# Moving GpSimd's tensor products to VectorE in a fused attention and two feed-forward kernel

## The chip, the cores and the metric

The kernel runs on one core of a Trainium2 chip. The metric is the device time of one execution in microseconds. TensorE does the matrix products, VectorE and GpSimd elementwise work, ScalarE activation functions and copies; SyncE issues most transfers. GpSimd can't read the accumulators (PSUM).

## What is computed

Three stages follow one another. All inputs are float32 (3072 tokens: 4 batches of 768).

```
# 1. a complex-decay recurrence over time, per batch and head (8 heads, D = 48)
scale = min(|a|, 0.999) / (|a| + 1e-6);  a_n = a * scale
S = a_n[t] * S + k[t] (outer) v[t]          # S complex, D x D, k v real
y[t] = q[t] @ real(S)
# 2. a feed-forward: 384 -> 2048 -> 384 with a parametric relu
h = x @ w_in;  x = (max(h, 0) + alpha * min(h, 0)) @ w_out
# 3. top-1 routing to 8 experts, 384 -> 1024 -> 384, relu
logits = x @ w_gate + bias[modality];  e = argmax;  out = p(e) * (relu(x @ w1[e]) @ w2[e])
```

## The kernel before

**Stage 1** is computed in chunks of 128 steps: 6 chunks by 4 batches are 24 steps k. The polar work turns the decay of two steps (a group, 128 partitions by 768 columns) into angles and magnitudes: `polar_group` (line 667). In its words: `ar`, `ai` are the parts of a, `q`, `kk` the queries and keys, and `m2`, `x`, `s`, `e` four work buffers with one slot each, so a new group waits for the slots of the one before. Squares and reciprocal roots (675 to 682), a range test (`ok`, 696 and 697), the arctangent (702), running products and sums over time (`scan`, 723), cosine and sine (748 to 751, tables loaded by ScalarE), then k times the inverse decay (752), q times the decay `pp` (754), and the rows of `z`: for the cosine (r = 0) and the sine (r = 1), k's row on VectorE (763) and q's row (765). `z` is written to DRAM (`zd`) and read back transposed (`qk`). The function `attn` (785) then makes scores (796), masks them (`at`, 798), multiplies with v and with the carried state (814, 816) and writes the transposed result `xt` (821).

Which engine takes an operation is decided by `side(mask)`: a group's `bit` is 1, 2, 4 and 8 for the first four (step 0, step 1, steps 2 and 3, steps 4 and 5) and 16 for all later groups; GpSimd takes the operation where mask and bit have a bit in common, else VectorE. With `GE`, `DQ` and `DZ` at 15, the groups from step 6 on (nine of them) have `ok` (696), q's decay (754) and both of q's rows (765) on GpSimd. For all groups from step 4 on, the cosine's q row is on GpSimd.

**Stage 2** is `moe1` (838): 12 units of 256 tokens, each 8 pairs p of hidden blocks; one pair is a turn g, 96 turns in all. Exactness comes from splitting float32 into an upper part (float32r) and the rest. `l1(g)` multiplies (857 to 860) into `ph`; ScalarE takes a relu (865) into `nf` (in the rows: n), VectorE completes the parametric relu with two instructions (867), ScalarE copies the upper part `gh` (870), and GpSimd makes the lower part `gl` = nf - gh (872). `l2(g - 2)` follows in the same turn: eight matmuls on gh, then four on gl (892), so a gl is read two turns after its first layer. `ph` and `nf` have two buffers, `gh` and `gl` three.

**The order of the work.** At the start a hand-written string orders the first polar groups, the decoding of the weights (`weights_part`, 547) and the first attention steps; in the first 14 turns a second list does so. From then on each unit of stage 2 carries the attention of the unit after it and the polar work of a later one, spread over 5 turns (u below 6) or 7 (later). The polar work of a turn is emitted `behind_turn` (161): `self.paced` holds three instructions of the turn, and with one engine asked for, VectorE's polar instructions are issued after the turn's last 867. What is emitted for the other engines is not held so. The instructions of an engine run in one fixed order that the scheduler of the tile framework chooses from emission order and readiness, not strictly the order of the code. `route` (230) takes the routing along, `ffn_load` (459) the weights of stage 3 (its weight differences are on GpSimd for every third block, `behind_turn` with all three instructions).

**Stage 3** is `moe2` (402), from about 712 us on.

Of the kernel before, what the change touches and what calls it, by code (L numbers as in the profile page):

```python
# [11 lines left out]
F32 = mybir.dt.float32  # L12
F32R = mybir.dt.float32r
BF16 = mybir.dt.bfloat16
I32 = mybir.dt.int32
AF = mybir.ActivationFunctionType
ALU = mybir.AluOpType
# [22 lines left out]
GHB = 3  # L40
# [7 lines left out]
AT = (1, 1, 2, 1, 1, 1, 1)  # L48
RT = ((3, 4), (3, 7))
WORK = "m2", "x", "s", "e"  # L50
XB = 2
PU = 7
KSB = 2
# [18 lines left out]
GB = 0  # L72
GC = 0
GD = 0
DQ = 15
DZ = 15
GE = 15
AS = 5
AE = 7
TM1 = 1  # L80
# [14 lines left out]
class Emit:  # L95
# [25 lines left out]
    def consts(self):  # L121
        nc, cp = self.nc, self.cp
        self.tiny = cp.tile([128, 1], F32, name="tiny")
        nc.vector.memset(self.tiny, 1e-25)
        warm = cp.tile([128, 1], F32, name="warm")
        nc.scalar.activation(warm, self.tiny, AF.Abs_reciprocal_sqrt)
        self.ident = cp.tile([128, 128], F32, name="ident")
        make_identity(nc, self.ident)
        self.mask = cp.tile([128, 128], F32, name="mask")
        nc.gpsimd.memset(self.mask, 1.0)  # L130
        nc.gpsimd.affine_select(
            out=self.mask, in_=self.mask, pattern=[[1, 128]], compare_op=ALU.is_ge,
            fill=0.0, base=0, channel_multiplier=-1,
        )
        self.hpi = cp.tile([128, 1], F32, name="hpi")
        nc.gpsimd.memset(self.hpi, math.pi / 2)
        self.mth = cp.tile([128, 1], F32, name="mth")
        nc.gpsimd.memset(self.mth, -0.56)

        self.first = {}  # L140
        for nm, at0, rest in (("angle", 0.0, 1.0), ("inverse", 1.0, 1e18), ("decay", 1.0, 0.0)):
            t = self.first[nm] = cp.tile([128, 3 * CH], BF16, name=f"first_{nm}")
            nc.gpsimd.memset(t, rest)
            nc.gpsimd.memset(t[:, ::CH], at0)
        self.carry = cp.tile([128, B, 3], F32, name="carry")
        self.magic = cp.tile([128, 1], F32, name="magic")
        nc.gpsimd.memset(self.magic, MAGIC)

        self.oks = cp.tile([128, NSTEP], F32, name="oks")
        nc.gpsimd.memset(self.oks, 2.0 * 3 * CH)  # L150
        self.pend = cp.tile([128, NSTEP, 3], F32, name="pend")
        self.state = cp.tile([96, B * H * D + 16], F32, name="state")
        nc.gpsimd.memset(self.state[:, B * H * D:], 0.0)
        self.al1 = cp.tile([128, NFC], F32, name="al1")
        one = self.one = cp.tile([128, 1], F32, name="one")
        nc.gpsimd.memset(one, 1.0)
        self.mhalf = cp.tile([128, 1], F32, name="mhalf")
        nc.gpsimd.memset(self.mhalf, -0.5)
        self.ones = one.to_broadcast([128, CH])
# [507 lines left out]
    def polar_group(self, ks, wa, wq, work, inline):  # L667
        nc, ap_ = self.nc, self.ap_
        c = ks[0] // B
        ar, ai, q, kk = wa[:, :, 0], wa[:, :, 1], wq[:, :, 0], wq[:, :, 1]  # L670
        m2, x, s, e = work
        V, G, A = nc.vector, nc.gpsimd, nc.scalar
        bit = {0: 1, 1: 2, 2: 4, 4: 8}.get(ks[0], 16)
        side = lambda mask: G if mask & bit else V
# [24 lines left out]
        yield 1  # L699
        V.scalar_tensor_tensor(s, e, 3.0, s, ALU.subtract, ALU.mult)  # L700
        yield 1
        A.activation(ai, ai, AF.Arctan)
        early = ks[0] < 4
        def scaled(bit, out, x, scale, bias):
# [133 lines left out]
    def moe1(self, units, emit_out, before=lambda g: None, after=lambda g: None, order=None, bank=None):  # L838


        nc, ap_, ps = self.nc, self.mp, self.ps
        gs, accs, xts = {}, {}, {}
        w1 = lambda fc, h, c: self.w[fc][:, h, 128 * c:128 * c + 128]
        order = order or [(j, p) for j in range(len(units)) for p in range(NP)]
        bank = bank or (lambda j, t: (ps, "acc", 2))

        def l1(g):
            j, p = order[g]
            u = units[j][0]
# [14 lines left out]
            nf = ap_.tile([128, 2, 256], F32, name=f"n{u}_{p}", tag="n", bufs=2)  # L864
# [3 lines left out]
                    nf[:, i, :], nf[:, i, :], self.al1[:, 2 * p + i:2 * p + i + 1], ph[:, i, :], ALU.mult, ALU.add).ins  # L868
            gh = ap_.tile([128, 2, 256], F32R, name=f"gh{u}_{p}", tag="gh", bufs=GHB)
            copy = nc.scalar.copy(gh, nf).ins  # L870
            gl = ap_.tile([128, 2, 256], F32R, name=f"gl{u}_{p}", tag="gl", bufs=GHB)
            rest = nc.gpsimd.tensor_tensor(gl, nf, gh.bitcast(F32), ALU.subtract).ins  # L872
            if self.pacing:
                self.paced = paced, copy, rest
            gs[g] = (gh, gl)

        def l2(g):
            j, p = order[g]
            u = units[j][0]
            if p == 0:  # L880
                accs[j] = []
                for t in range(2):
                    pool, tag, bufs = bank(j, t)
                    accs[j].append(pool.tile([128, 512], F32, name=f"acc{u}_{t}", tag=tag, bufs=bufs))
            acc = accs[j]
            gh, gl = gs.pop(g)
            pieces = [(t, i, gh, h) for i in range(2) for t in range(2) for h in range(2)]
            pieces += [(t, i, gl, 0) for i in range(2) for t in range(2)]
            if p == NP - 1 and TM1:
                pieces.sort(key=lambda x: x[0])  # L890
            for t, i, x, h in pieces:
                nc.tensor.matmul(acc[t][:, :XW], x[:, i, 128 * t:128 * t + 128], self.w[2 * p + i][:, h, DM:],  # L892
                                 start=(p == i == h == 0 and x is gh), stop=(p == NP - 1 and i == 1 and x is gl))

        n = len(order)
        for g in range(n + LAG):
# [3 lines left out]
            if g >= LAG:  # L900
                l2(g - LAG)
                j, p = order[g - LAG]
# [492 lines left out]
```

## Time and profile before

| | us |
|---|---|
| three runs | 945.52, 948.34, 954.92 |
| median | 948.34 |
| the profiled execution | 951.42 |
| its span, first to last instruction | 949.6 |

The profile is of one execution on this core. Busy time of an engine is the time covered by its instructions; PE is TensorE (PEld its weight loads), DVE VectorE, ACT ScalarE, POOL GpSimd, SP SyncE. Matmuls overlap in their pipeline, so a duration of one is longer than the distance to the next. "Idle before <-X" is how long the engine had nothing to do before an instruction, and which instruction released it. The granted clock (PEclk) is 1.00 at 2.4 GHz and 0.50 at 1.2 GHz.

### The profile page before, as it was taken

The numbers are of one execution on the slowest core, as the hardware profiler recorded it, in microseconds if no ns is written. First come the engines' busy times: TensorE is split into PE (matmuls) and PEld (weight loads), VectorE is DVE, ScalarE is ACT, GpSimd is POOL, SyncE is SP. The second block draws the span as 40 slices with busy tenths as digits, with TensorE's granted clock in tenths as the row PEclk, the third lists the DMA queues.
The fourth block names the chain that finished last, engine by engine and source line by source line (L and its number), as shares of the span: only waits on it lengthen the run. The fifth ranks groups of instructions, "written<-read, shape, count | busy, mean of one in ns | idle before, by whom it ended". The sixth has DMA issues, their size and how long they took to land.

```text
span 949.6 us, 16186 instructions
## 1 busy us (share of the span) xinstructions
PE 838.5 (88%) x5948; PEld 798.2 (84%) x5948; DVE 649.6 (68%) x1268; ACT 479.2 (50%) x870; POOL 397.9 (42%) x335
## 2 busy tenths in 40 slices
PE   0767969889889899998989998989999999999994
PEld 0656958878889899998989998989998879899993
DVE  7878886896779595969687877924555644435551
ACT  7744556664655464655554656422334433434550
POOL 2003543436355346454635464532443335334550
PEclk9856988889899999999999999999999999999997
DMA  8728400444562722425252526150214455435560
GB/s 316 251 83 278 149 10 1 146 118 105 139 180 65 180 65 78 149 71 171 61 142 94 149 70 174 65 105 26 79 41 135 117 169 167 132 109 180 178 195 19
DMA packets 61289, 117.81 MB, mean 124 GB/s; under 512 B 10200, under 2 KB 39400, under 8 KB 61200
## 3 DMA queue, kind: packets, MB, share of 16 engines
q1 hardware_dynamic: 57232, 106.91, 38.2%
q0 software_dynamic: 3968, 9.77, 3.3%
q8 instruction: 49, 0.80, 0.4%
q14 instruction: 40, 0.33, 0.1%
HBM read 85.58 MB, written 28.91 MB: 121 GB/s over the span
## 4 chain that ended last, share of the span: by engine, by line
PE 38%; DVE 20%; DMA 12%; issue 11%; POOL 5%; ACT 4%; SPq 0%; POOLq 0%; DVEq 0%; ACTq 0%
PE acc L892 7%; DMA qk<-zd 7%; PE a2s L498 6%; DMA zd<-z 4%; PE ph L857 3%; PE pa L796 3%; PE ph L858 3%; DVE n L867 3%; PE ph L860 3%; DVE z L763 2%; PE p2s L483 2%; PE p2s L479 2%; PE p2s L480 2%; POOL gl L872 1%; POOL wq L754 1%
## 5 line engine op out<-in xcount | busy, mean ns | idle before, releaser
L872 POOL TENSOR_TENSOR gl<-n,gh 128x512 fp32r<-128x512 f32 x96 | 150.9, 1573 | 208.1 <-ACT gh L870 100.3
L857 PE MATMUL ph<-xt,w 128*128 128x256 f32 x576 | 159.9, 304 | 14.2 <-DVE n L867 12.4
L892 PE MATMUL acc<-w,gh 128*128 128x392 f32 x768 | 160.5, 347 | 0.0
L858 PE MATMUL ph<-xt,w 128*128 128x256 f32 x576 | 153.3, 293 | 0.0
L867 DVE SCALAR_TENSOR_TENSOR n<-n,al,ph 128x256 f32<-128x256 f32 x192 | 84.3, 474 | 97.2 <-ACT n L865 96.9
L892 PEld LDWEIGHTS acc<-w,gh 128*128 128x128 f32 x768 | 134.8, 191 | 0.8 <-issue 0.7
L857 PEld LDWEIGHTS ph<-xt,w 128*128 128x128 f32 x576 | 115.6, 201 | 16.6 <-DVE n L867 7.0
L858 PEld LDWEIGHTS ph<-xt,w 128*128 128x128 f32 x576 | 115.7, 201 | 0.2 <-issue 0.2
L860 PE MATMUL ph<-xt,w 128*128 128x256 f32 x576 | 105.3, 293 | 4.1 <-DVE w L560 4.1
L870 ACT CAST gh<-n 128x512 fp32r<-128x512 f32 x96 | 59.4, 618 | 86.1 <-DVE n L867 71.1
L860 PEld LDWEIGHTS ph<-xt,w 128*128 128x128 f32 x576 | 87.2, 200 | 4.5 <-DVE w L560 4.3
L892 PE MATMUL acc<-w,gl 128*128 128x392 f32 x384 | 87.7, 344 | 3.1 <-POOL gl L872 3.0
L865 ACT ACTIVATE n<-ph 128x512 f32<-128x512 f32 x96 | 56.8, 592 | 61.3 <-PE ph L860 54.1
L796 PE MATMUL pa<-qk 96*128 96x128 f32 x384 | 58.7, 301 | 23.2 <-DMA qk<-zd 20.8
L796 PEld LDWEIGHTS pa<-qk 96*128 96x128 f32 x384 | 54.3, 212 | 27.1 <-issue 21.8
L892 PEld LDWEIGHTS acc<-w,gl 128*128 128x128 f32 x384 | 70.1, 190 | 3.7 <-POOL gl L872 3.7
L798 DVE TENSOR_TENSOR at<-pa,mask 128x512 f32<-128x512 f32 x48 | 32.6, 680 | 25.9 <-PE pa L796 19.8
L584 POOL TENSOR_TENSOR w<-of,w 128x8 fp32r<-128x8 f32 x16 | 10.1, 652 | 92.6 <-ACT w L583 92.6
L487 DVE SCALAR_TENSOR_TENSOR hls<-p2s,hhs 128x512 fp32r<-128x512 f32 x32 | 22.0, 688 | 38.5 <-ACT hhs L486 38.5
L814 PE MATMUL py<-at,v 128*64 128x128 f32 x384 | 43.6, 300 | 3.3 <-DVE at L798 3.3
L468 DVE TENSOR_TENSOR wls<-wrs,whs 128x768 fp32r<-128x768 f32 x20 | 28.6, 1432 | 25.6 <-ACT whs L467 25.6
L261 POOL DMA_INDIRECT tbl<-tok,ix x24 | 24.9, 1037 | 49.7 <-DVE ix L259 43.3
(333 smaller groups left out, 2023.4 us busy)
## 6 DMA issues: line engine op xcount, KB each, us to landing
zd<-z SPq DMA_DIRECT2D x24, 771.0 KB, 3.7
qk<-zd SPq DMA_DIRECT2D x24, 771.0 KB, 7.0
wraw<-in_w_io_dram SPq DMA_DIRECT2D x16, 768.0 KB, 11.9
wrs<-in_wcat_dram SPq DMA_DIRECT2D x32, 384.0 KB, 3.2
wrf<-in_wcat_dram SPq DMA_DIRECT2D x24, 384.0 KB, 3.8
wa<-in_pa__dram SPq DMA_DIRECT2D x10, 768.0 KB, 4.5
wq<-in_pq__dram SPq DMA_DIRECT2D x10, 768.0 KB, 9.6
v<-in_vv_dram SPq DMA_DIRECT2D x24, 200.0 KB, 4.9
```

The lines of the kernel that those rows point to most:

```text
L498: nc.tensor.matmul(acc[t], x[:, 128 * t:128 * t + 128], w[:, DM:], start=(f == 0 and x is hh and w is wh), stop=(last and x is hl))
L796: nc.tensor.matmul(pa[:, i, :], kt[:, h, :], qt[:, h, :CH], start=True, stop=True)
L798: self.last = nc.vector.tensor_tensor(at, pa, self.mask.unsqueeze(1).to_broadcast([128, 4, CH]), ALU.mult).ins
L814: nc.tensor.matmul(o, v[:, h * D:h * D + 64], ats[g][:, i, :], start=True, stop=(c == 0))
L857: nc.tensor.matmul(ph[:, i, :], w1(fc, 0, c), xt[:, c, 0, :], start=(c == 0), stop=False)
L858: nc.tensor.matmul(ph[:, i, :], w1(fc, 0, c), xt[:, c, 1, :], start=False, stop=False)
L860: last = nc.tensor.matmul(ph[:, i, :], w1(fc, 1, c), xt[:, c, 0, :], start=False, stop=(c == 2)).ins
L865: nc.scalar.activation(nf, ph, AF.Relu, scale=-1.0)
L867: paced = nc.vector.scalar_tensor_tensor(nf[:, i, :], nf[:, i, :], self.al1[:, 2 * p + i:2 * p + i + 1], ph[:, i, :], ALU.mult, ALU.add).ins
L870: copy = nc.scalar.copy(gh, nf).ins
L872: rest = nc.gpsimd.tensor_tensor(gl, nf, gh.bitcast(F32), ALU.subtract).ins
L892: nc.tensor.matmul(acc[t][:, :XW], x[:, i, 128 * t:128 * t + 128], self.w[2 * p + i][:, h, DM:], start=(p == i == h == 0 and x is gh), sto ...
```

## The change

It has four parts. `gl` of a turn is made on VectorE instead of GpSimd, and one turn later, behind the two 867 of the next turn; the last one is made in `l2`. `self.paced` then holds this late `gl`, so VectorE's polar work stands behind it. `GE`, `DQ` and `DZ` are 31, which takes `ok`, q's decay and the sine's q row to VectorE in the nine later groups; the cosine's q row stays on GpSimd. Every second group, from step 6 on, uses the slots of `s` and `e` the other way round. And ScalarE evaluates a sine of one column into a scratch tile just ahead of the arctangent.

```
+TURNED = "m2", "x", "e", "s"
...
-DQ = 15
-DZ = 15
-GE = 15
+DQ = 31
+DZ = 31
+GE = 31
...
+        self.trig = cp.tile([128, 1], F32, name="trig")
...
-        m2, x, s, e = work
+        m2, x, s, e = (work[WORK.index(t)] for t in (TURNED if ks[0] // 2 % 2 and ks[0] > 3 else WORK))
...
+        A.activation(self.trig[:, :1], ai[:, 0, :1], AF.Sin)
         A.activation(ai, ai, AF.Arctan)
...
+        late = []
+        def lower(engine, g, nf, gh, u, p):
+            gl = ap_.tile([128, 2, 256], F32R, name=f"gl{u}_{p}", tag="gl", bufs=GHB)
+            gs[g] = (gh, gl)
+            return engine.tensor_tensor(gl, nf, gh.bitcast(F32), ALU.subtract).ins
...
             copy = nc.scalar.copy(gh, nf).ins
-            gl = ap_.tile([128, 2, 256], F32R, name=f"gl{u}_{p}", tag="gl", bufs=GHB)
-            rest = nc.gpsimd.tensor_tensor(gl, nf, gh.bitcast(F32), ALU.subtract).ins
+            rest = None
+            if True:
+                parts = late.pop() if late else None
+                late.append((g, nf, gh, u, p))
+                if parts:
+                    paced = lower(nc.vector, *parts)
+                rest = paced
+            else:
+                rest = lower(nc.gpsimd, g, nf, gh, u, p)
             if self.pacing:
                 self.paced = paced, copy, rest
-            gs[g] = (gh, gl)

         def l2(g):
+            if g not in gs:
+                lower(nc.vector, *late.pop())
```

## Rows read from the trace of the kernel before

**Rows 1.** The page's busy times: engine, busy us, share of the span, instructions.

```profile
PE 838.5 (88%) x5948; PEld 798.2 (84%) x5948; DVE 649.6 (68%) x1268; ACT 479.2 (50%) x870; POOL 397.9 (42%) x335
```

**Rows 2.** TensorE's waits, 250 to 712 us: total us, times, longest.

```profile
PE pa L796 <- DMA qk<-zd: 19.6, 7, 3.7
PE py L814 <- DVE at L798: 3.3, 1, 3.3
```

**Rows 3.** Stretches of 50 us: PE, PEld, DVE, ACT, POOL busy, PEclk, DMA.

```profile
150.00:200.00 50.00, 42.04 (x264) 40.48 (x264) 44.33 (x57) 33.76 (x57) 17.66 (x15) 0.86 0.33 95
250.00:300.00 50.00, 46.27 (x391) 44.88 (x390) 41.22 (x69) 29.94 (x53) 24.82 (x18) 0.97 0.45 123
600.00:650.00 50.00, 46.61 (x364) 45.44 (x363) 27.04 (x63) 16.64 (x32) 22.05 (x16) 0.97 0.32 77
```

**Rows 4.** The same view over one unit of eight turns.

```profile
413.80:463.50 49.70, 47.12 (x373) 46.10 (x375) 38.41 (x77) 28.59 (x49) 24.49 (x20) 0.97 0.42 117
```

**Rows 5.** The chain that ended last, 417 to 431 us: start, us, what.

```profile
417.43 1.64 DVE z L763
...
419.22 3.51 DMA zd<-z
...
422.75 7.79 DMA qk<-zd
```

**Rows 6.** Timeline of TensorE, 409 to 431 us: start, us, instruction, idle before.

```profile
409.02 0.52 PE L860 MATMUL ph<-xt,w 128*128 128x256 f32 x3
...
417.29 0.88 PE L892 MATMUL acc<-w,gl 128*128 128x392 f32 x4
...
430.68 1.51 PE L796 MATMUL pa<-qk 96*128 96x128 f32 x8 [2.58 <-DMA qk<-zd]
```

**Rows 7.** Timeline of GpSimd, 408 to 431 us.

```profile
408.62 1.96 POOL L872 TENSOR_TENSOR gl<-n,gh 128x512 fp32r<-128x512 f32 x1 [4.69 <-issue]
410.55 1.82 POOL L754 TENSOR_TENSOR wq<-wq,m 128x768 f32<-128x768 f32 x1
...
429.42 1.27 POOL L872 TENSOR_TENSOR gl<-n,gh 128x512 fp32r<-128x512 f32 x1 [0.89 <-DVE n L867]
```

**Rows 8.** Line 872, 80 to 230 us: ns min/median/max, first and last start.

```profile
L872 POOL TENSOR_TENSOR gl<-n,gh x17: 1279/1869/5390, 84.7 to 229.3; 128x512 fp32r<-128x512 f32 x17
```

**Rows 9.** ScalarE's waits, 250 to 620 us: total us, times, longest.

```profile
ACT m L676 <- POOL wq L754: 14.1, 7, 2.2
```

**Rows 10.** Timeline of ScalarE, 413 us.

```profile
413.16 0.58 ACT L865 ACTIVATE n<-ph 128x512 f32<-128x512 f32 x1
```

**Rows 11.** Timeline of VectorE, 413 to 432 us.

```profile
413.84 0.87 DVE L867 SCALAR_TENSOR_TENSOR n<-n,al,ph 128x256 f32<-128x256 f32 x2 [3.76 <-ACT n L865]
414.63 1.59 DVE L752 TENSOR_TENSOR wq<-wq,s 128x768 f32<-128x768 f32 x1
...
428.50 0.95 DVE L678 TENSOR_TENSOR m<-m,e 128x768 f32<-128x768 f32 x1
429.48 2.02 DVE L684 TENSOR_TENSOR e<-wa,x 128x768 f32<-128x768 f32 x1
```

**Rows 12.** VectorE by line, 413.8 to 463.5 us: busy us, mean ns, idle before.

```profile
L763 DVE TENSOR_TENSOR z<-wq,x 128x384 f32<-128x384 f32 x2 | 2.2, 1092 | 0.0
...
L711 DVE SCALAR_TENSOR_TENSOR m<-m,s 128x768 f32<-128x768 f32 x1 | 1.9, 1917 | 0.0
```

**Rows 13.** VectorE by line, 0 to 84 us.

```profile
L763 DVE TENSOR_TENSOR z<-p,p 128x384 f32<-128x384 f32 x4 | 2.2, 546 | 0.0
```

**Rows 14.** TensorE's waits, 100 to 250 us.

```profile
PE ph L857 <- DVE n L867: 12.4, 4, 3.8
PE acc L892 <- POOL gl L872: 3.0, 1, 3.0
```

**Rows 15.** Timeline of ScalarE, 23 us.

```profile
23.00 1.28 ACT L750 ACT_TABLE_LOAD   x1
```

**Rows 16.** Timeline of VectorE, 25 us.

```profile
24.95 0.56 DVE L763 TENSOR_TENSOR z<-wq,e 128x384 f32<-128x384 f32 x1 [1.26 <-ACT e L750]
```

## The prediction

> **What bounds the kernel now.** I read the page's busy shares first: TensorE's matmuls are busy 838.5 us of the 949.6 us span [rows 1], more than any other engine. TensorE leads, so a change on VectorE and GpSimd can only pay where TensorE stands still or runs at its lower clock. The second view is TensorE's waits by releaser. From 250 to 712 us, where the first feed-forward and the attention run interleaved, nearly all of its idle time has one name: the score matmuls waiting for the transfer qk, 19.6 us in seven waits, the longest 3.7; one more wait of 3.3 us is for the masked scores on VectorE [rows 2]. The third view, stretches of 50 us, shows a granted clock of 0.97 in six of the nine between 250 and 700 us, the first and the last of the six in [rows 3]: after such a stop the engine runs some microseconds at 1.2 GHz, then at 2.4 again. 0.03 of 50 us is 1.5 us of lost work, six times: 9 us.
>
> The fourth view, one period of eight turns (a unit: two steps of attention), gives the load: in 49.7 us TensorE is busy 47.1, VectorE 38.4, GpSimd 24.5 [rows 4].
>
> **Why qk is late.** The chain of waits ends with the last z row on VectorE (417.43 to 419.07), the write of z to DRAM (3.51) and the read back (7.79), and then the scores [rows 5]. TensorE started them at 430.68 after 2.58 idle, so it stood still from 428.10 [rows 6]. Why does that z row end at 419? GpSimd computes q's decay (L754) from 410.55 to 412.37, and only after the gl (L872) that was in front of it, 1.96 long where the shortest takes 1.28 [rows 7, 8]. ScalarE's first square of the next group (L676) writes into the buffer that L754 reads, so it waits for it, and behind it in ScalarE's queue stands the relu of the next turn, which starts at 413.16 although its ph was complete at 409.54 (409.02 plus 0.52) [rows 6, 10]. The two n instructions of that turn follow at 413.84, and behind them, by the pacing edge, k's product at 414.63 and the z rows [rows 11]. That wait of ScalarE on L754 comes seven times between 250 and 620 us, 14.1 us in all and 2.2 at most [rows 9].
>
> **The change, part by part.** All sums are against the profiled execution, 951.4 us with 949.6 in the span; the median of the three runs is 948.3, so 3.1 comes off at the end.
>
> *q's decay on VectorE.* L754 now stands behind the n pair and k's product on VectorE, so the next group's square can no longer be queued in front of a relu that L754 itself waits behind. The relu starts at about 409.6, the n pair ends 1.5 later (as 413.16 to 414.63 did) at 411.1, the late gl at 411.7. Then k's product and q's decay, 0.87 apart each (a product of 768 columns left alone takes 0.95, and neighbours overlap by 0.08, as the n pair from 413.84 for 0.87 and its follower at 414.63 do [rows 11]), three rows of z at 0.47, and a microsecond because GpSimd keeps q's first row: z is complete at about 415.8 instead of 419.07, 3.3 us earlier. Of seven waits of at most 3.7 that removes nearly all; but the margin over the 2.58 is only 0.7, so I leave 2.6 standing: minus 17. With the stops go their half-clock stretches: minus 7 of the 9. What is late next is VectorE itself, so of the 3.3 on the masked scores I take 1.
>
> *What VectorE pays.* A 128x512 product of two SBUF operands is not in its trace. It lies between 0.55 (384 columns) and 0.95 (768) [rows 11, 13], by interpolation 0.68, 0.60 apart in a queue. A unit gets eight of them (4.8), the range test's product and q's decay (0.87 each), two q rows (0.47 each): plus 7.5 us. Against it, GpSimd's operations stretch VectorE's today: L684 takes 2.02, L711 1.92, L763 with the sine 1.09 twice [rows 11, 12], while a product of the same size left alone takes 0.95 and 0.55: 1.07 + 0.97 + 1.09 = 3.1 us a unit. Rows of the same kind that I don't count stand against the GpSimd work that stays (q's first rows, the state product, one scaling). So 38.4 + 7.5 - 3.1 = 42.8 us, while the unit would shrink to some 45.7 (49.7 less 2.6 and 1.5): 94% busy, now 77%. It fits, but an instruction that TensorE needs is behind more of a queue. The late gl, done at about 411.7 in the turn above, is read by matmuls that start at 417.29 today [rows 6]: 5.6 us of cover, some two less in a turn without attention work. A polar turn in which VectorE falls further behind than that stops TensorE. The late gl also frees n's buffer: the relu two turns on waits for it on ScalarE, with the copy gh and the polar activations queued behind, and the polar work of a turn is held behind the gl as well. I charge half a microsecond for each of eight to nine units: plus 4 (bounds 0, and the whole of rival C).
>
> *The start, before 230 us.* There VectorE decodes the weights and is the engine that others wait for: 44.3 of 50 us at 150 to 200 [rows 3]; TensorE waits 12.4 us for n in four places and 3.0 for a gl on GpSimd [rows 14]. The 3.0 goes. The 17 gl that start before 230 [rows 8] put 17 x 0.60 = 10.2 us more on VectorE; it counts fully only where TensorE waits for n, with one or two gl in front of each of the four waits, so I take 4 between minus 10 (if each of the 17 now delays VectorE by as much as it would cost it) and plus 10.2.
>
> *After 712 us* the second feed-forward has no gl; only its first weight differences on GpSimd lose their place behind gl: 0.
>
> *The tiny sine ahead of the arctangent.* Today each group loads a table before the arctangent and another before the sine, 1.28 us each. At the start one such load stands on the path: ScalarE loads at 23.00, and VectorE's first z row waits 1.26 for the cosine [rows 15, 16]. If one table holds both, that is minus 1.3; if the arctangent evicts the sine's, one more load comes in each group, and ScalarE, busy 28.6 of 49.7 [rows 4], hides it except at the start, plus 1.3. No row tells which, so I take 0. *The swapped buffers* of every other group let the next group's first square start before the last z row; only ScalarE gains, which is not the limit: 0.
>
> Sum: -17 - 7 - 1 + 4 - 3 + 4 = -20, so 931.4 for an execution like the profiled one and about 928 for the median.
>
> **Two rules of the notes.** VectorE's L684 took 2.02 us from 429.48, where the product of the same size just before it took 0.95 [rows 11], and GpSimd ran a gl from 429.42 for 1.27 [rows 7]. The Trainium skill, "SBUF — State Buffer", section "Who interferes with whom", says that a VectorE instruction with two SBUF inputs and a GpSimd instruction that reads SBUF exclude each other for the whole instruction. The trace agrees. By that rule alone every removed gl would free VectorE, and the 7.5 would be met by more than the 3.1 that I count.
> Against the change speaks the Trainium skill, "Perfetto Trace Analysis", section "Optimizing Scalar/DVE Operations": where VectorE is saturated, work may go from it to other engines. At 42.8 of 45.7 us it is nearly so here; what this would do in this kernel is rival C.
>
> **The rivals.**
> *A, everything goes.* All 19.6 of the qk waits, all 9.0 of the clock, 3.3 for the masked scores, 3.0 for the gl, and no new wait: 34.9, so 916.5, or 913 on the median's scale. For it: the waits are all of one kind, and none is longer than 3.7. Against: a margin of 0.7 us.
> *B, the transfer comes no earlier.* The late gl, the extra product and the extra row in front of z eat the 3.3 us, or another ScalarE instruction takes the square's place ahead of the relu. Then only the start counts: -3 + 4, so 952, or 949. For it: the order on an engine is the scheduler's, and no row shows the new one.
> *C, VectorE becomes the bound, slower.* If its instructions stay as long as they are, a unit holds 38.4 + 7.5 = 45.9 us of VectorE. It stands idle 11.3 of 49.7 today, waiting on relus and scores; if half of that stays, the unit takes 51.5, 1.8 more, nine times 16; the start pays 10.2 and gains 3.0. Plus 23: 974, or 971. It decides from about 44 us of VectorE per unit. For it: 44.3 of 50 us in the start already. Against: 3.1 us of stretched instructions in three rows.
>
> **How the numbers follow.** The forecast has 0.47 (own range 918 to 937), A 0.20, B 0.21, C 0.12. One per cent of 948 is 9.5 us, about what a measurement of this kernel can tell from no change. Forecast and A are faster by more: 0.67; B is the same: 0.21; C slower: 0.12. The range goes from A less its unknowns (half of the 10 at the start, 1.3 of the table) at 906 up to B plus its table load and the 3.0 if that wait stays too, 953; C is left out.
>
> **What would show it.** Right: no wait of TensorE on qk above 1 us between 250 and 640, a clock of 1.00 in most stretches of 50 us, the relu at the end of a polar group starting within 0.3 us of its ph, L684 and L711 near 1 us, VectorE at 41 to 44 us per unit, GpSimd under 8. Wrong: waits of TensorE on n or gl that total more than 10 us after 250; the waits on qk still there; L684 still at 2 us without a gl beside it.

## The result and the profile after

The changed kernel takes 910.25 us (median of four runs, 907.61 to 912.2) where the kernel before, in the same comparison, takes 946.93: a ratio of 0.960 [0.953, 0.966] (in brackets, here and below, the 95% interval). The forecast was 928, or 0.979. The profiled execution after is 910.59 us with a span of 908.8, against 951.42 and 949.6. The line numbers move: in after the relu is L878, the pair on n L880, gl L858, k's product L757, q's decay L759, the rows of z L768 and L770, the scores L801.

Busy times of after, which answer to [rows 1]:

```profile
PE 819.3 (90%) x5948; PEld 780.0 (86%) x5948; DVE 662.5 (73%) x1400; ACT 467.4 (51%) x871; POOL 205.7 (23%) x203
```

GpSimd's work is halved, VectorE's grows by only 13 us although 132 instructions came to it, and TensorE does the same work in 19 us less: it runs less at its lower clock. 7.7 of these lie ahead of its first turn (28.43 and 20.75 in the first lines of the windows below).

TensorE's waits of after from 250 to 712 us, as in [rows 2]; it is the only row that the view has:

```profile
PE pa L801 <- DMA qk<-zd: 11.4, 4, 5.6
```

The waits on qk fall from 19.6 to 11.4 us, the 3.3 us for the masked scores are gone, and no wait on n or gl came in their place.

To see where the rest comes from, the two spans are cut at the same events: the first product of ph in turns 0, 16, 28 and 80 of the first feed-forward, and its end. Columns as in [rows 3]. First the kernel before:

```profile
0.00:63.60 63.60, 28.43 (x174) 26.32 (x175) 48.63 (x80) 40.32 (x74) 4.93 (x31) 0.83 0.69 241
63.60:223.00 159.40, 128.73 (x878) 120.83 (x878) 131.77 (x205) 90.54 (x171) 66.13 (x56) 0.84 0.35 107
223.00:304.90 81.90, 73.57 (x580) 70.96 (x580) 69.03 (x123) 48.55 (x84) 40.16 (x28) 0.94 0.51 136
304.90:629.00 324.10, 304.08 (x2463) 295.91 (x2461) 246.96 (x495) 174.90 (x299) 160.65 (x124) 0.98 0.41 113
629.00:711.10 82.10, 81.79 (x606) 79.55 (x604) 38.13 (x137) 26.16 (x47) 29.54 (x25) 0.98 0.19 52
```

The same stretches of after:

```profile
0.00:56.20 56.20, 20.75 (x175) 19.24 (x175) 50.00 (x82) 41.12 (x79) 4.90 (x31) 0.98 0.78 273
56.20:206.40 150.20, 125.85 (x876) 117.80 (x877) 131.02 (x213) 85.62 (x167) 26.40 (x36) 0.86 0.37 114
206.40:286.60 80.20, 73.39 (x581) 70.04 (x582) 71.43 (x150) 48.82 (x86) 16.28 (x14) 0.94 0.55 136
286.60:589.30 302.70, 296.90 (x2465) 290.29 (x2462) 253.34 (x574) 166.93 (x295) 52.54 (x42) 1.00 0.47 124
589.30:669.30 80.00, 80.00 (x605) 78.10 (x604) 41.62 (x153) 26.38 (x47) 10.42 (x10) 1.00 0.15 44
```

Turns 28 to 80 give 21.4 us: TensorE's idle time there goes from 20.0 (324.10 less 304.08) to 5.8, and its clock from 0.98 to 1.00, by which its busy time falls by 7.2. Turns 0 to 16 give 9.2. The 7.4 us ahead of turn 0 are not put down to the change: the clock of that stretch (0.83 and 0.98) follows none of its parts. Of the kernels below two, only_masks and only_pair, take about as long as the kernel before (63.2 and 64.3 us to turn 0), while the other sixteen take 55.9 to 58.8, among them only_decay and load_more, which have little or nothing of the change. The second feed-forward is unchanged (238.4 and 239.4 us). Turns 28 to 80 are therefore the stretch by which the experiments are read: nothing of the start is in it. Each such window is of one execution, and executions of one kernel differ (the kernel before took 937.5 to 952.9 us in thirteen of them), so a few us in one window show a cause only together with the ratio.

### The profile page after: what moved, and what is told of

The parts are those of the page before. It is cut to its first block, busy times and chain, and to the rows that moved or that the text cites. A ratio compares the mean times of both kernels' runs of the same rounds, so it can differ in the third digit from the quotient of the medians.

```text
span 908.8 us, 16009 instructions
## 1 busy us (share of the span) xinstructions
PE 819.3 (90%) x5948; PEld 780.0 (86%) x5948; DVE 662.5 (73%) x1400; ACT 467.4 (51%) x871; POOL 205.7 (23%) x203
## 4 chain that ended last, share of the span: by engine, by line
PE 51%; DVE 14%; DMA 10%; issue 4%; ACT 1%; POOL 1%; SPq 0%; POOLq 0%; DVEq 0%; ACTq 0%
PE acc L913 12%; PE a2s L500 6%; DMA qk<-zd 5%; PE ph L870 4%; PE ph L871 4%; PE ph L873 4%; DMA zd<-z 3%; PE pa L801 3%; PE p2s L485 2%; PE p2s L481 2%; DVE n L880 2%; PE p2s L482 2%; PE pu L833 2%; PE py L819 1%; PE a2t L500 1%
## 5 line engine op out<-in xcount | busy, mean ns | idle before, releaser
L870 PE MATMUL ph<-xt,w 128*128 128x256 f32 x576 | 155.3, 298 | 9.7 <-DVE n L880 5.0
L871 PE MATMUL ph<-xt,w 128*128 128x256 f32 x576 | 149.6, 288 | 0.0
L870 PEld LDWEIGHTS ph<-xt,w 128*128 128x128 f32 x576 | 112.0, 194 | 11.6 <-DVE n L880 5.5
L880 DVE SCALAR_TENSOR_TENSOR n<-n,al,ph 128x256 f32<-128x256 f32 x192 | 84.0, 473 | 43.9 <-ACT n L878 43.8
L871 PEld LDWEIGHTS ph<-xt,w 128*128 128x128 f32 x576 | 112.2, 195 | 0.2 <-issue 0.2
L873 PE MATMUL ph<-xt,w 128*128 128x256 f32 x576 | 103.2, 288 | 3.5 <-DVE w L562 3.5
L878 ACT ACTIVATE n<-ph 128x512 f32<-128x512 f32 x96 | 56.9, 593 | 72.0 <-PE ph L873 69.9
L858 DVE TENSOR_TENSOR gl<-n,gh 128x512 fp32r<-128x512 f32 x96 | 66.4, 691 | 30.2 <-ACT gh L883 29.4
L873 PEld LDWEIGHTS ph<-xt,w 128*128 128x128 f32 x576 | 84.7, 195 | 3.7 <-DVE w L562 3.7
L263 POOL DMA_INDIRECT tbl<-tok,ix x24 | 27.4, 1141 | 200.7 <-DVE ix L261 191.0
L801 PE MATMUL pa<-qk 96*128 96x128 f32 x384 | 55.2, 288 | 15.0 <-DMA qk<-zd 13.1
L801 PEld LDWEIGHTS pa<-qk 96*128 96x128 f32 x384 | 51.5, 201 | 18.3 <-DMA qk<-zd 8.6
L500 PE MATMUL a2s<-whs,hhs 128*128 128x384 f32 x128 | 43.7, 341 | 0.0
L500 PE MATMUL a2s<-wls,hhs 128*128 128x384 f32 x128 | 43.5, 340 | 0.0
L469 ACT CAST whs<-wrs 128x768 fp32r<-128x768 f32 x32 | 26.3, 833 | 32.3 <-PE a2s L500 15.8
```

Source lines behind the costliest of these rows:

```text
L263: nc.gpsimd.indirect_dma_start(out=self.tbl, out_offset=bass.IndirectOffsetOnAxis(ap=ix, axis=0), in_=self.tok[:, c, b, :], in_offset=None ...
L500: nc.tensor.matmul(acc[t], x[:, 128 * t:128 * t + 128], w[:, DM:], start=(f == 0 and x is hh and w is wh), stop=(last and x is hl))
L801: nc.tensor.matmul(pa[:, i, :], kt[:, h, :], qt[:, h, :CH], start=True, stop=True)
L858: return engine.tensor_tensor(gl, nf, gh.bitcast(F32), ALU.subtract).ins
L870: nc.tensor.matmul(ph[:, i, :], w1(fc, 0, c), xt[:, c, 0, :], start=(c == 0), stop=False)
L871: nc.tensor.matmul(ph[:, i, :], w1(fc, 0, c), xt[:, c, 1, :], start=False, stop=False)
```

## The experiments

Each kernel below is the kernel before with one part added, or the changed kernel with one part undone. "28 to 80" is the time from TensorE's first product of ph in turn 28 to that in turn 80 (before 324.1, after 302.7); "qk" is TensorE's wait on qk from 250 to 712 us (before 19.6, after 11.4). The two don't always go together: only_gl has short waits on qk and a long stretch, load_more waits as little as only_sine and takes 5.8 us more.

| kernel | ratio to before | qk | 28 to 80 |
|---|---|---|---|
| only_sine | 0.987 [0.981, 0.993] | 13.9 | 311.4 |
| load_early | 0.992 [0.988, 0.995] | 13.2 | 311.7 |
| load_more | 1.000 [0.995, 1.004] | 13.5 | 317.2 |
| only_gl | 0.990 [0.986, 0.995] | 6.5 | 320.4 |
| only_masks | 1.004 [1.000, 1.007] | 20.6 | 322.8 |
| only_decay | 1.008 [1.003, 1.014] | 20.3 | 320.5 |
| decay_held | 0.995 [0.991, 1.000] | 15.1 | 311.5 |
| only_pair | 0.980 [0.975, 0.985] | 13.5 | 311.2 |
| less_sine | 0.974 [0.968, 0.980] | 13.6 | 308.7 |
| less_gl | 0.990 [0.983, 0.998] | 17.3 | 316.5 |
| less_masks | 0.981 [0.975, 0.987] | 9.4 | 311.9 |
| less_turned | 0.967 [0.961, 0.973] | 7.3 | 302.8 |
| same_turn | 1.006 [1.002, 1.010] | 26.8 | 328.1 |
| same_free | 0.977 [0.972, 0.983] | 11.9 | 304.4 |
| all_rows | 0.952 [0.946, 0.958] | 3.4 | 300.2 |
| rows_scale | 0.952 [0.946, 0.958] | 3.9 | 300.7 |
| after_held | 0.965 [0.957, 0.972] | 6.9 | 299.4 |
| rows_held | 0.953 [0.946, 0.961] | 3.5 | 299.4 |

### The sine ahead of the arctangent

```
+        A.activation(self.trig[:, :1], ai[:, 0, :1], AF.Sin)
         A.activation(ai, ai, AF.Arctan)
```

Added alone to the kernel before:

> The kernel before with the tiny sine ahead of the arctangent and nothing else of the change. Theory S (the sine decides the start): each group has two table loads in place of three, the first scores start 1.2 us earlier, and because TensorE is then busy a little sooner its clock stays at 2.4 GHz past 42 us, where it fell to 1.2 before; the relu of turn 0 starts at about 68 us in place of 76.1, and the time falls by 8 us (ratio 0.991). Rival T (a load is worth itself): two loads in place of three, 1.3 us, the clock of the start as before, turn 0 at about 75, ratio 0.998 to 1.000.

Undone in the changed kernel:

> The changed kernel without the tiny sine. Theory S: the start is as in the kernel before, turn 0 at about 76 us, clock down from 42 us on; 8 us slower than the changed kernel, ratio to the kernel before 0.969. Rival T: 1 to 2 us slower than the changed kernel, ratio 0.962.

Alone it gives 1.3 per cent, and its loss takes 1.4 points from the change (0.974 against 0.960). The table loads of the kernel before ahead of the arctangent (L702) and the cosine (L750), over the whole run:

```profile
L702 ACT ACT_TABLE_LOAD x12 | 15.4, 1283 | 0.2
L750 ACT ACT_TABLE_LOAD x12 | 15.4, 1283 | 0.2
```

With the sine (L706 in only_sine) one row stands for both:

```profile
L706 ACT ACT_TABLE_LOAD x12 | 15.4, 1283 | 0.2
```

Alone, the gain is not at the start. Turn 0 does begin 6.8 us earlier, as the first theory had it, but so it does in kernels without the sine (55.9 in only_decay, 56.4 in less_sine); turns 0 to 16 take 160.5 us with it and 159.4 without, while turns 28 to 80 lose 12.7. In the changed kernel turns 28 to 80 take 6.0 us less by it and turns 0 to 16 4.2 (308.7 and 154.4 in less_sine, 302.7 and 150.2 after). The place is the end of a polar group. ScalarE of the kernel before (timeline):

```profile
402.22 0.83 ACT L748 ACTIVATE e<-x 128x768 f32<-128x768 f32 x1
...
403.43 1.28 ACT L750 ACT_TABLE_LOAD   x1
404.73 0.94 ACT L750 ACTIVATE e<-e,hpi 128x768 f32<-128x768 f32 x1
405.57 0.83 ACT L751 ACTIVATE x<-x 128x768 f32<-128x768 f32 x1
406.31 0.57 ACT L865 ACTIVATE n<-ph 128x512 f32<-128x512 f32 x1
```

The same group with the sine alone added:

```profile
393.66 0.83 ACT L753 ACTIVATE e<-x 128x768 f32<-128x768 f32 x1
...
394.76 0.94 ACT L755 ACTIVATE e<-e,hpi 128x768 f32<-128x768 f32 x1
395.60 0.83 ACT L756 ACTIVATE x<-x 128x768 f32<-128x768 f32 x1
396.33 0.58 ACT L878 ACTIVATE n<-ph 128x512 f32<-128x512 f32 x1
```

From the Abs to the relu of the turn it was 4.09 us and is 2.67: the load stood in ScalarE's queue ahead of a relu. The load itself costs the 1.30 from its start to the cosine's. The Trainium skill, "ScalarE: Activation LUTs", section "What ACT_TABLE_LOAD costs", puts a drain of about 1.38 us on top of it, which this trace doesn't show. Behind that relu stand the pair on n (406.91), ScalarE's copy gh (done at 408.49) and the gl at 408.62 [rows 7], which stood in front of the decay; from there the chain is that of the prediction's account. The five waits on qk between 350 and 600 us fall from 12.4 to 6.4 us in all.

Is it that a load is gone, or where it stood? Two kernels ask. load_early has the sine behind the arctangent, with three loads as before, and load_more another activation ahead of the cosine, with a fourth:

```
         A.activation(ai, ai, AF.Arctan)
+        A.activation(self.trig[:, :1], ai[:, 0, :1], AF.Sin)
```

```
+        A.activation(self.trig[:, :1], e[:, 0, :1], AF.Abs_reciprocal_sqrt)
         A.activation(cs, e, AF.Sin, bias=self.hpi, scale=-2.0 * PI_LO)
```

> The kernel before with the sine of one column just behind the arctangent in place of ahead of it: three table loads a group as before, but the last of them is moved from ahead of the cosine to behind the arctangent, some turns earlier. If the place of the load ahead of a turn's relu is what costs, this gains as much as the sine ahead of the arctangent did (0.987): a ratio of 0.982 to 0.994, with turns at the end of a polar group 1.3 to 1.4 us shorter. If the number of loads counts, nothing: 0.996 to 1.004.

> The kernel before with a reciprocal root of one column just ahead of the cosine: ScalarE loads a table more in each group (the one of the root between the arctangent's and the sine's), 1.28 us each, four loads a group in place of three. If what the sine ahead of the arctangent brought (0.987) is the place of one load in ScalarE's queue, this costs as much the other way: a ratio of 1.008 to 1.02, and the waits of TensorE on qk after 250 us grow above 20 us. If the load was covered and the sine's gain was the start alone, 0.998 to 1.005.

load_early keeps three loads, moves one some turns ahead, and gains the same 12 us in turns 28 to 80: there the place counts, not the number. As a ratio it gives 0.8 per cent where the sine gives 1.3; the intervals overlap, so that the missing load is worth something too is not excluded. load_more was to cost as much and cost nothing. Its ScalarE:

```profile
399.81 1.28 ACT L751 ACT_TABLE_LOAD   x1
401.10 0.20 ACT L751 ACTIVATE trig<-e 128x1 f32<-128x1 f32 x1
401.32 1.28 ACT L753 ACT_TABLE_LOAD   x1
402.62 0.84 ACT L753 ACTIVATE x<-x 128x768 f32<-128x768 f32 x1
403.37 0.58 ACT L867 ACTIVATE n<-ph 128x512 f32<-128x512 f32 x1
403.84 0.93 ACT L752 ACTIVATE e<-e,hpi 128x768 f32<-128x768 f32 x1
```

The scheduler put the cosine behind the relu: the relu comes 4.77 us after the Abs (398.60), 0.68 more than before, and not 1.5 more. So the cost could only be half of what was expected; but a relu that is later still should have cost something, and turns 28 to 80 take 6.9 us less than before. This run doesn't confirm the account by the load's place, and why it is not dearer is open. The account rests on only_sine, less_sine and load_early.

### The decay, the masks and the order on SP's queue

The decay alone, and (only_masks) DZ and GE at 31 with it:

```
-DQ = 15
+DQ = 31
```

> The kernel before with q's decay alone on VectorE for the nine later groups. Theory M: this one product holds the square, the relu and so the z rows, so it gives most of what the three products give: 12 us less (ratio 0.987), no wait of ScalarE's first square on it. Rival P: 2 us or less (ratio 0.998 to 1.002).

> The kernel before with the range test's product, q's decay and the sine's q row on VectorE for the nine later groups, gl left on GpSimd. Theory M: the wait of ScalarE on the decay is gone, most of the waits of TensorE on qk (19.6 us from 250 to 712 us) with it; 16 us less (ratio 0.983). Rival P: gl still excludes VectorE, which has more to do now; between no change and 6 us less (ratio 0.994 to 1.000).

ScalarE's wait on GpSimd's decay [rows 9] is gone in both, as the forecast had it, and the waits on qk stay at 20 us. In only_decay the first step's z does come earlier. SyncE's issues in the kernel before, around the chain of [rows 5]:

```profile
419.22 0.32 SPq L662 DMA_DIRECT2D zd<-z  x1
420.46 1.53 SPq L823 DMA_DIRECT2D xt<-t  x2
422.75 0.33 SPq L662 DMA_DIRECT2D qk<-zd  x1
423.20 0.46 SPq L662 DMA_DIRECT2D zd<-z  x1
```

and in only_decay, where the scores begin at 429.75 in place of 430.68:

```profile
416.10 0.32 SPq L664 DMA_DIRECT2D zd<-z  x1
417.56 1.54 SPq L827 DMA_DIRECT2D xt<-t  x2
419.32 0.59 SPq L664 DMA_DIRECT2D zd<-z  x1
420.01 6.83 SPq L664 DMA_DIRECT2D qk<-zd  x2
```

The first write starts 13.65 us ahead of the scores, before 11.46. The second step's z is ready early too, and its write goes ahead of the first step's read back, where before it was issued 0.45 us behind it. Of the chain's last pieces in only_decay

```profile
420.01 9.61 DMA qk<-zd
```

is 1.8 us longer than the 7.79 of [rows 5]. In the mean of the last six groups of turns 28 to 80 it is less: from the first write's start to the read back's end 12.0 us before, 13.0 in only_decay. A kernel with the old order forced onto that queue tests this: the read back of the first step is emitted first, and the second write and the load of wq are issued after it.

```
-BB = 1
+BB = 0
...
-        self.dma(zd.rearrange("h (p c) t -> (h p) (c t)", c=6), z.rearrange("p c j t -> p (c j t)"))
+        with self.tc.issue_after(self.back) if self.back and k % 2 else nullcontext():
+            self.dma(zd.rearrange("h (p c) t -> (h p) (c t)", c=6), z.rearrange("p c j t -> p (c j t)"))
...
```

> The kernel before with q's decay alone on VectorE (1.008, 20.3 us of waits on qk), and on SP's queue the order that the kernel before shows: write of the first step's z, its read back qk, then the second step's write and the load of wq. In the run without this order the first z was complete 2.5 us earlier against the turns, but the second step's write went ahead of the read back, and the way from z to the scores took 13.68 us in place of 11.62. If this sharing is what ate the gain, the waits on qk fall below 12 us and the ratio is 0.980 to 0.995; if not, the waits stay near 20 us and the ratio between 1.00 and 1.015.

The waits fall to 15.1 us only, but the mean way from write to read back is 12.3 us, the ratio goes from 1.008 to 0.995, and turns 28 to 80 from 320.5 to 311.5. Windows of only_decay, then of decay_held:

```profile
304.90:625.40 320.50, 303.61 (x2464) 295.30 (x2462) 253.01 (x496) 175.97 (x298) 153.71 (x117) 0.98 0.45 117
```

```profile
300.50:612.00 311.50, 299.26 (x2464) 290.83 (x2461) 252.42 (x488) 174.37 (x298) 154.85 (x117) 1.00 0.42 117
```

So by these windows the decay on VectorE is worth 12.6 us of that stretch, and the order on SP took back 9.0 of it. Clear of noise is the order (1.008 [1.003, 1.014] against 0.995 [0.991, 1.000]); whether the second write or the load of wq does it is not told apart, as the edit moves both. Against the kernel before the ratio shows little of the 12.6, because turns 16 to 28 take 88.1 us here (87.5 in only_decay) and 81.9 before. Part of the way can stay long even so: in one group, with no second write ahead of it, the read back is issued 5.98 us after the first write (406.41 and 412.39), in the kernel before 3.53. These runs leave that open. In the changed kernel the second write is again issued ahead of the read back:

```profile
391.19 0.51 SPq L664 DMA_DIRECT2D zd<-z  x1
```

Its chain of waits there:

```profile
387.30 0.56 DVE z L770
...
388.01 8.46 DMA zd<-z
...
396.54 6.96 DMA qk<-zd
...
403.63 0.46 PE pa L801 x2
```

From the last row of z (387.86) to the scores it is 15.8 us; before it was 11.6. Here it is the first write that is longer, 8.46 us against 3.51, not the read back, and the order is not enough to explain it: of the 16 parts in which that write lands, the trace has 14 by 391.44, when the second write had only just been issued, and the last two at 393.38 and 396.48. The old order was tried here as well:

> The changed kernel with that same order on SP's queue. Its first z is complete 9.08 us ahead of the scores' turn, where it was 4.61, but the way to the scores took 15.77 us. With the order held it should take about 11.6 again, so that the waits on qk after 250 us (11.4 us in four) go but for the one near 259: a ratio of 0.950 to 0.960, 0 to 1 per cent under the changed kernel. If the waits are not from the order, 0.957 to 0.966.

The waits fall from 11.4 to 6.9 us, the mean way from 13.3 to 12.1, and the time doesn't (0.965 [0.957, 0.972] against 0.960). With no second write ahead of the read back the first write still takes 6.8 to 7.3 us in three of the last six groups. Why the last parts of a write land late in some groups is open.

### gl and the masks together

only_gl adds the late gl alone, only_pair the late gl and the masks. The other two undo a part of the changed kernel, less_gl by the first edit and less_masks by the second:

```
-            if True:
+            if False:
```

```
-DQ = 31
-DZ = 31
-GE = 31
+DQ = 15
+DZ = 15
+GE = 15
```

> The kernel before with the lower parts of the first layer on VectorE one turn later and nothing else of the change. Theory M (q's decay on GpSimd makes qk late): the decay stays on GpSimd, but no gl is in front of it any more, so about a third to a half of the 19.6 us of waits on qk goes; in the decoding stretch from turn 9 to 23 the waits for GpSimd and the stretched instructions go, 8 us; total 14 us less (ratio 0.985). Rival P (GpSimd and VectorE exclude each other, and that is all there is): nearly the whole gain, 25 us or more (ratio under 0.974).

> The changed kernel with gl on GpSimd in its own turn as before; the masks, the swapped buffers and the sine stay. Theory M: 8 from the start (sine) and 16 from the masks remain, ratio to the kernel before 0.975; the stretch from turn 9 to 23 takes as long as before. Rival P: 8 from the start and at most 6 more, ratio 0.986 or above.

> The changed kernel with the range test's product, q's decay and the sine's q row back on GpSimd. Theory M: the waits on qk are back in part (8 to 12 us from 250 us on), ratio to the kernel before 0.976. Rival P: gl is gone from GpSimd, so next to nothing is lost, ratio 0.964.

> The kernel before with two parts of the change together: the lower part gl on VectorE one turn later, and the three masks at 31. No sine, buffers not swapped. Alone the first gave a ratio of 0.990 and the second 1.0035, which multiply to 0.994. If the parts act by themselves, the ratio is 0.99 to 1.00 and TensorE's waits on qk after 250 us stay above 6 us. If GpSimd must be left by both at once, the ratio is 0.965 to 0.98, that of the whole change without the sine (0.974), and the waits on qk after 250 us are below 6 us in all.

Alone they give 0.990 and 1.004, together 0.980: the parts don't add. Undone in the changed kernel they cost 3.0 points (gl) and 2.1 (the masks). With gl still on GpSimd (only_masks), VectorE's rows of z are stretched by gl and by the q row behind it. The sine's q row, which is new on VectorE, as min/median/max ns of 14, in only_masks and then in only_pair:

```profile
L769 DVE TENSOR_TENSOR z<-wq,x x14: 546/961/1657, 304.1 to 616.4; 128x384 f32<-128x384 f32 x14
```

```profile
L769 DVE TENSOR_TENSOR z<-wq,x x14: 547/552/1377, 301.5 to 597.0; 128x384 f32<-128x384 f32 x14
```

The first write of z is longer in only_masks too, 5.3 to 6.6 us in its last six groups (3.51 in [rows 5]); its cause is not shown. With the masks at 15 and gl gone (only_gl), ScalarE waits 17.2 us for GpSimd's range test product (8.0 before) and 10.1 for its decay (14.1 before) from 250 to 620 us, and TensorE gets waits for the masked scores, 13.8 us in 16 (4.2 in two before). Only when both leave is VectorE mostly left alone. Mean durations of three of its instructions in turns 28 to 80 of the kernel before:

```profile
L726 DVE TENSOR_TENSOR_SCAN s<-first_inverse,s 128x384 f32<-128x384 bf16 x12 | 17.1, 1466 | 0.0
L684 DVE TENSOR_TENSOR e<-wa,x 128x768 f32<-128x768 f32 x6 | 12.1, 2020 | 0.2
L752 DVE TENSOR_TENSOR wq<-wq,s 128x768 f32<-128x768 f32 x6 | 9.9, 1645 | 0.0
```

and of the lines that answer to them in after, where every second group uses e for s:

```profile
L858 DVE TENSOR_TENSOR gl<-n,gh 128x512 fp32r<-128x512 f32 x53 | 36.8, 694 | 16.6 <-ACT gh L883 16.5
L731 DVE TENSOR_TENSOR_SCAN s<-first_inverse,s 128x384 f32<-128x384 bf16 x6 | 5.7, 946 | 0.0
L687 DVE TENSOR_TENSOR e<-wa,x 128x768 f32<-128x768 f32 x3 | 2.9, 958 | 0.1
L757 DVE TENSOR_TENSOR wq<-wq,s 128x768 f32<-128x768 f32 x3 | 2.9, 950 | 0.0
```

VectorE's busy time in turns 28 to 80, 6.5 units of eight turns, goes from 246.96 to 253.34: 1.0 us a unit.

### The delay of gl by a turn

In the changed kernel gl goes back into its own turn. same_turn is shown; same_free leaves `paced` at the pair on n.

```
-                parts = late.pop() if late else None
-                late.append((g, nf, gh, u, p))
-                if parts:
-                    paced = lower(nc.vector, *parts)
-                rest = paced
+                rest = paced = lower(nc.vector, g, nf, gh, u, p)
```

> The changed kernel with gl on VectorE in its own turn, right behind the two instructions on n, in place of one turn later. VectorE then waits in its queue for ScalarE's copy gh (0.5 to 0.6 us) in each of 96 turns, and what stands behind it waits along. If that wait counts in full in half of the 88 turns, the ratio to before goes from 0.96 to about 0.985 and TensorE gets waits on n or at. If VectorE's idle time covers it, 0.955 to 0.965, and the delay of a turn is worth nothing.

> The changed kernel with gl on VectorE in its own turn, but with the polar work of the turn held behind the two instructions on n and not behind gl. With both in its own turn the ratio was 1.006. If what is lost there is that the polar work stood behind a gl that waits for ScalarE's copy, this is like the changed kernel: 0.955 to 0.968, with waits of TensorE on qk after 250 us of 6 us or less. If gl itself must come a turn later in VectorE's queue, it stays near 1.006 (0.99 to 1.01) with waits on qk above 15 us.

In its own turn the move loses everything: 1.006. VectorE of same_turn:

```profile
402.74 0.87 DVE L880 SCALAR_TENSOR_TENSOR n<-n,al,ph 128x256 f32<-128x256 f32 x2 [0.28 <-ACT n L878]
404.35 0.69 DVE L858 TENSOR_TENSOR gl<-n,gh 128x512 fp32r<-128x512 f32 x1 [0.74 <-ACT gh L883]
404.96 0.95 DVE L757 TENSOR_TENSOR wq<-wq,e 128x768 f32<-128x768 f32 x1
```

The polar work (k's product, L757) is held behind the paced instruction, here a gl that waits 0.74 us for ScalarE's copy: 2.2 us after the start of the pair, where in only_masks it was 0.8. In the changed kernel it is held behind the gl of the turn before. With the edge left at n (same_free) most comes back: turns 28 to 80 fall from 328.1 to 304.4, 1.7 us from the changed kernel. On the engine itself the late gl is hardly late: in after 73 of 96 gl still start ahead of the next turn's relu, many right behind their own copy, as the 16.5 us of waits on gh in the row of L858 above show. The delay pays mainly by what it lets past, not by where gl runs. As a whole same_free stays 1.7 points behind (0.977); most of that lies in turns 16 to 28 and 80 to 96 (84.7 and 85.6 us against 80.2 and 80.0), and its cause is open.

### The swapped buffers

```
-TURNED = "m2", "x", "e", "s"
+TURNED = WORK
```

> The changed kernel with all groups using the work buffers in one order. If the swapped buffers only let ScalarE square earlier, as I took it, the ratio to the kernel before stays 0.960 (within 0.003). If they carry part of the gain, because the next group's first square no longer waits for the last z row and the polar work of the next group starts earlier, 5 us or more are lost, ratio 0.965 or above.

0.967 [0.961, 0.973] against 0.960 [0.953, 0.966], and 302.8 us against 302.7 in turns 28 to 80: no effect that these runs can tell, although the waits on qk are 4 us shorter without it.

### Further in the same direction

all_rows takes the cosine's q rows to VectorE in the changed kernel; rows_scale adds the last scaling, to ScalarE (the second edit), and rows_held the order on SP.

```
-                side(~(15 if ks[0] < 4 else DZ if r else 0)).tensor_tensor(z[:, r, :, :CH], t3(q[:, i]), t3(tr[:, i]), ALU.mult)
+                side(~(15 if ks[0] < 4 else DZ)).tensor_tensor(z[:, r, :, :CH], t3(q[:, i]), t3(tr[:, i]), ALU.mult)
```

```
-AS = 5
+AS = 7
```

> The changed kernel with the last regular tensor products of GpSimd, the cosine's q rows from step 4 on, on VectorE too: two rows a unit, about 0.5 us each, and one us less of GpSimd ahead of the write of z. If VectorE at 41 to 44 us in 50 is near its bound, the time goes up by 0.5 to 1.5 per cent against the changed kernel (ratio to before 0.965 to 0.975), with waits of TensorE on n, at or gl. If there is room, it is the same or up to 0.5 per cent faster (0.955 to 0.962).

> The changed kernel with the cosine's q rows on VectorE (0.952) and the last scaling of GpSimd, L711, on ScalarE as well: one instruction of 768 columns a group, 0.94 us on ScalarE. If GpSimd beside VectorE still stretches VectorE, the gain goes on: 0.944 to 0.951. If ScalarE's queue ahead of the relu is now the nearest limit, it is the same or slower: 0.951 to 0.962.

> The same order on top of the kernel with all q rows on VectorE (0.952, waits on qk of 3.4 us after 250 us). Little is left to gain: 0.946 to 0.954 if the order only removes those waits; above 0.956 if holding the second write back makes the second step's scores late.

With the cosine's q rows on VectorE too, the median is 900.19 us, 0.952 [0.946, 0.958], ahead of both kernels by its median, though its interval still meets the changed kernel's. Of the 13.7 us between the two spans, 9.3 lie in turns 16 to 28 (70.9 against 80.2), where the wait of 5.6 on qk goes, and 2.5 in turns 28 to 80 (that profiled execution is the fastest of its four, 896.88 us). The two additions bring nothing more: neither the last scaling on GpSimd nor the order on SP is seen to limit it.

## Why the prediction came out short

The measured time lies below the forecast's own range (918 to 937). The spans differ by 40.8 us where 20 were forecast: 7.4 ahead of turn 0 (0 forecast), 9.2 in turns 0 to 16 (forecast 1 the other way), 25.2 from turn 16 to the end of the first feed-forward (21), and 1.0 lost after it.

**The step that failed.** "The tiny sine ahead of the arctangent. ... No row tells which, so I take 0", with 1.3 at most and "ScalarE ... hides it except at the start". Measured: 1.3 per cent alone, 1.4 points in the change, some 13 us by the ratios and 9.9 between the two spans (918.7 and 908.8). Both halves of the step were wrong: one table serves the sine and the arctangent, and ScalarE's idle share does not hide a load that stands in its queue ahead of a relu, as far as only_sine, less_sine and load_early show it (load_more does not). The row was there to be read: the load at 403.43 stands between the Abs and the relu of 406.31, the same place that the prediction found for the square behind the decay. Without the sine the change gives 0.974 [0.968, 0.980], and the forecast's 0.979 lies within that, but partly by luck, as the next terms show.

**The waits on qk, -17, and the clock, -7.** The clock was about right: TensorE's busy time in turns 28 to 80 falls by 7.2, without the sine by 4.4. The waits on qk were not: from 250 to 712 us they fall by 8.2, from 19.6 to 11.4, and without the sine by 6.0. What made up for it are terms that came out better than forecast: the masked scores, VectorE's new waits, the start. The mechanism of the decay holds (ScalarE's wait on it is gone; decay_held, 12.6 us in its window), but the forecast let the transfer follow z at the old length, and in the changed kernel the way from the first write to the read back's end is 13.3 us in the mean instead of 12.0, in the group shown 4.2 us longer from z to the scores. Part of that is the order on SP (12.1 with the old one), part the late ends of the first write, whose cause is open. That is rival B's thought, in a place that B did not name: not ahead of z but behind it. In only_decay, by its window, the order took back most of the gain; in the whole change it cost nothing that can be measured.

**Rival A** named 913 us, nearer to the measured 910 than the forecast. Its ground, that all the waits go, is not what happened: 11.4 us of them stayed, and the sine, which A left out, and the earlier turns 0 to 16 made up for it.

**VectorE's new waits, +4, and its load.** No wait of TensorE on n or gl is seen after 250 us, so 0. The load was to grow by 7.5 - 3.1 = 4.4 us a unit and grew by 1.0, so that 6.5 came back and not 3.1: the scan L726 and the products L686 and L752 were stretched as well, not L684, L711 and L763 alone. By the Trainium skill, "SBUF — State Buffer", section "Who interferes with whom", a VectorE instruction with two SBUF inputs and a GpSimd instruction that reads SBUF contend for a port pair that is locked for one of them; the prediction noted that by this rule more than 3.1 would come back, and the trace agrees with the rule: 2.02 to 0.96 us for L684, 1.65 to 0.95 for k's product. Rival C, VectorE as the bound, had its point at 44 us a unit; VectorE is at 39.0 (253.34 over 6.5) of 46.6.

**The start, -3 + 4.** The 3.0 us on GpSimd's gl went, and the waits on n [rows 14] fell from 12.4 us in place of growing. The view of TensorE's waits from 100 to 250 us has in after:

```profile
PE ph L870 <- DVE n L880: 5.0, 2, 3.2
```

Turns 0 to 16 take 9.2 us less, 4.2 of them by the sine. They take 154.4 in less_sine and 156.4 in only_gl, and VectorE is busy there for 131.0 us after and 131.8 before, so the lower parts are at least not dearer on VectorE there. How the rest divides is open, since the clock in that stretch differs between executions.

**The masked scores, -1,** gave 3.3: the wait has no row in after. **The swapped buffers, 0:** right. **After 712 us, 0:** right (+1.0).

**The signs.** Clock 1.00 in most stretches: right from turn 28 on. L684 and L711 near 1 us: right. GpSimd under 8 us a unit: 52.54 over 6.5 is 8.1, nearly. No wait on qk above 1 us: wrong (5.6, 2.9 and 2.3). VectorE at 41 to 44 us per unit: wrong, 39.0. The relu at the end of a polar group within 0.3 us of its ph: wrong. It starts at 384.19, 1.4 us after ph (382.30 plus 0.52), because the square now waits for the decay on VectorE; before it was 3.6.

## To carry to other kernels

When one instruction in an in-order queue is found to stand ahead of the path, price everything else that stands there, a table load too, before it is taken as hidden by the engine's idle share. When data become ready earlier, read the whole queue of transfers behind them: a second transfer that also becomes ready can go in front (1.008 against 0.995 with the order held). Parts of a change that take the same engine out of the way do not add, and an edge that orders work can be worth more than the instruction that it is tied to: here 2.9 points (1.006 against 0.977) hung on which instruction the polar work was held behind.

## What the runs showed of the hardware that was not expected

- A table loaded ahead of a sine serves the arctangent that follows and the later sine; one loaded ahead of the arctangent does not serve the sine. The loads per group went from three to two (37 to 25 in all), each 1.28 us.
- The read back took 7.79 us where the second write was issued 0.45 us behind it, and 9.61 where it was issued 0.69 ahead of it. The first write of z took 3.51 us in one group and 8.46 in another, 14 of its 16 parts landing within 3.4 us in the second.
- VectorE's scan L726 took 1466 ns in the mean of twelve in the kernel before, and 946 in the changed kernel, where less of GpSimd's work runs beside it.
